# A softcap attention and a mixture of attention experts on one core: one batch's second score slot a step sooner, the second head pair's operands copied out in three pieces, and other constants in the order's search

## The chip, the cores and the metric

The kernel runs on one core of a Trainium2 chip. A core has a matrix engine (TensorE; PE in the profile, its weight loads PEld), a vector engine (VectorE, DVE), a scalar engine for activation functions (ScalarE, ACT), a general engine (GpSimd, POOL) and a queue engine that starts most transfers (SyncE, SP). The metric is the device time of one execution in microseconds (us); less is better. Of several runs of a kernel the median counts.

## The reference

Attention with a soft cap comes first, for 8 batches of 12 heads, 448 positions and 64 numbers a head:

```python
scores = q @ k.T / 8
scores = cap * tanh(scores / cap)          # cap = 30
attn = exp(scores - max) / sum             # over the keys
x = attn @ v                               # then heads side by side: (8, 448, 768)
```

Its output is the input of a mixture of four attention experts with 64 numbers each. A gate (x by a 768 x 4 matrix) picks two experts for each position, with weights w0 and w1 from a softmax over the two; each expert is a causal attention over x with projections of its own:

```python
for e in range(4):
    q, k, v = x @ wq[e], x @ wk[e], x @ wv[e]
    a = softmax(causal(q @ k.T / 8))
    out += weight_of_e * (a @ v) @ wo[e]   # weight 0 where e isn't chosen
```

So each score of the first attention costs ScalarE a tanh and an exp, and each of the second costs an exp. The experts of a batch need all twelve heads of that batch.

## The kernel before, in words

**Heads in pairs.** The 96 heads are taken as 48 pairs p = 0 to 47, six pairs a batch. The last batch begins with pair 42. For each of its pairs only the first 320 rows of queries are done pair by pair; the last 128 rows of all six come as two further steps, p = 48 and p = 49, called groups here, with three pairs each.

For each p the scores are filled into PSUM by TensorE in three parts, by chunks of keys. X is the first 128 keys of both heads and the tails (the last 64 keys of both heads side by side), Y1 and Y2 the second and third 128 keys of both. ScalarE takes a tanh of each part as it copies it to SBUF (`tanh`, line 842). Then one exp runs over the whole pair (`expo`, line 854). X owns three PSUM banks and Y two, so a part can be filled only when the tanh of what was there before is done. `fill` gives these matmuls (lines 789 in `heads` and 799 in `tails`). In general Y2 of pair p and X of pair p + 1 are filled by one operation of the program. The set `alone` lists the p for which they are two operations: pair 0, and every p with a slot (below).

Before a pair's scores can be filled, its operands must be brought: loads by SyncE, casts to 16 bits on GpSimd and VectorE (`cast`; the keys' tail is the cast at line 681), TensorE's transposes, and VectorE's copies to the tile qk (`tr`; keys 512 columns and queries 448 columns, 960 in all). Pair 0 has a branch of its own with several copies (lines 724 and 761). For the others up to pair 33 all transposes go to one PSUM bank and one copy of 960 columns follows (line 752). `setup_v` zeroes the padding of the value tiles (the memsets at lines 526 to 531).

After the exp of a pair, TensorE does its product with the values (`pv`, lines 869 and 877), VectorE normalises (lines 898 and 901) and the result is transposed (`xt`) to xT, the experts' input.

**The experts of a batch** are worked in beside the next batch's pairs: `b_v` (values and gate), `b_qk` (queries and keys), `b_gate`, `b_mask`. A batch has two *slots* of scores, s = 0 and 1: for each position the first chosen expert and the second, with the queries of the others masked to zero. `b_score` fills 18 matmuls into two of the X banks (line 1158), and one exp on ScalarE (line 1167) takes them; then come ten products with the values (`b_pv`, line 1217), the normalising with the gate's weights (line 1232), a sum of the two slots and transposes (`b_ot`) and the output projection (`b_wo`, line 1279; two matmuls make one pair for half of 128 rows, copied out at line 383). Slots stand at offsets 5 and 6 from the batch's end: for batch b at p = 6(b + 1) + 5 and + 6. Batch 6 has offsets 5 and 7 by the table `late`, so p = 47 and p = 49.

In the loop over p, the order of ScalarE's work at a step with a slot is: tanh of X and Y1 of p, the exp of pair p - 1, the slot's exp, tanh of Y2 of p. So a fixed chain of ScalarE's instructions is written down by the order of the calls.

**The last batch's experts** have no pairs to stand beside. `last` does the first 320 rows (projections line 1372, scores 1401, exp 1430, products 1458), with ScalarE and VectorE sharing the copies. `last2` does the last 128 rows (scores 1518, products 1572). `normed` normalises a block of 128 rows (lines 1308 to 1316), transposes it to oTL, does the output projection (line 1345) and the stores (lines 1354 to 1361).

**The planner.** No instruction is issued as the functions run. They record operations in a `Graph`, with the engine, an estimated duration, what is read and written, and PSUM groups. `dues` gives each operation a due time backwards from ScalarE's chain; some calls state it as an offset from a tanh (the pairs `(ref, offset)`). `solve` (line 134) then simulates the engines and issues in the order that results. On each engine it takes among the operations that can start within `near` the one that ranks first (`rank`, line 190). Score fills, transposes and a few others are `first`: ranked by their due times as they are, while all others are ranked no earlier than 1.097 us from now. A group already begun gets a bonus of 0.796, a second half-array matmul (scores) one of 2.0. `SEEDS` and `JIT` shift the ranks by a pseudo-random amount for each 4 us. At the end, a `first` operation that can start soon passes ahead of the one chosen if it would be due within 0.433 us of that one's end (line 206):

```python
for t2, u in c:
    if u.first and u.due + lag < t + o.occ + 0.433 and t2 < t + (
            o.occ if early else max(SWITCH + 0.01, min(o.occ, 0.25))):
        t, o = t2, u
        break
```

All this happens while the program is built; the chip sees only the order on each engine and the waits.

Of the kernel before, what the change touches and what calls it, by code (L numbers as in the profile page):

```python
# [18 lines left out]
TAIL = 4  # L19
LAND = 2.942  # L20
LAND0 = 2.314
FLIGHT = 8
JIT = 0.377
SEEDS = (0, 0, 0, 641, 0, 564, 447, 0, 424, 0, 460, 0, 235, 957, 407, 782, 983, 0, 912, 404, 0, 970, 362, 0, 379, 864, 0, 72, 966, 0, 904, 104, 0, 980, 497, 974, 196, 827, 159, 0, 805, 165, 0, 235, 0, 755, 596, 262, 998, 26, 102, 0, 0, 552, 777, 594, 0, 873, 143, 97, 0, 0, 943, 0, 690, 925, 0, 147, 0, 0, 0, 830, 464, 0, 0, 0, 267, 0)
TWIRE = 0.1
# [28 lines left out]
class Graph:  # L54
# [79 lines left out]
    def solve(self, when, banks, lent):  # L134
# [44 lines left out]
        while len(order) < n:  # L179
            best = None  # L180
            for e, rs in ready.items():
                if not rs:
                    continue
                c = [(est(o, e), o) for o in rs if e == o.eng or not left]
                if not c:
                    continue
                t0 = min(x[0] for x in c)
                if t0 >= INF or (best is not None and t0 >= best[0]):
                    continue
                def rank(x):  # L190
                    u = x[1]
                    if u.name[:4] == "gexp":
                        return -INF, 0.0, 0
                    d = u.due + lag if u.first or left < TAIL else max(u.due + lag, t0 + 1.097)
                    d -= 0.796 * (u.grp is not None and not u.opens and left >= TAIL)
                    k = SEEDS[int(t0 / 4.0)] if t0 < 4.0 * len(SEEDS) else 0
                    if k:
                        d += ((u.idx * 40503 + k * 9973) % 1009 / 1009.0 - 0.5) * JIT
                    return d - 2.0 * (u.half == 1 and half == 1), u.due, u.idx

                near = t0 + (0.005 if left >= TAIL else SWITCH + 0.02)
                t, o = min((x for x in c if x[0] <= near), key=rank)
                early = e == "POOL" and t < HEAD
                if (e in ("PE", "DVE") or early) and not o.first:
                    for t2, u in c:
                        if u.first and u.due + lag < t + o.occ + 0.433 and t2 < t + (
                                o.occ if early else max(SWITCH + 0.01, min(o.occ, 0.25))):
                            t, o = t2, u
                            break
                if best is None or t < best[0]:  # L210
                    best = (t, e, o)
# [64 lines left out]
def kernel(  # L276
# [85 lines left out]
    def bank16(g):  # L362
        return BANK[g.bank].bitcast(f16)
# [331 lines left out]
    def tr(p):  # L695
# [19 lines left out]
        if p == 0:  # L715
# [10 lines left out]
                name="qk0")  # L726
            return
        g = Group(AUX)
        if p >= KD:
# [12 lines left out]
            return  # L742
        pe(0, lambda: tk(g, (0, 1, 2)), kr + [("s", XB[0])] * (p == 1), [("tps", p, "k"), ("qkw", t)], g, occ=0.165, name=f"trk{p}")
        m, kx = (4, (-1,)) if p == 1 else (2, ())
        pe(0, lambda: (tq(g, 0, m), None if kx else tk(g, (-1,))),
           [("q16", i), "ident"] + (ktr if not kx else []),
           [("tps", p, "q")], g, occ=0.2 if kx else 0.15, name=f"trq{p}",
           due=5.0 if p == 1 else None)
        pe(0, lambda: tk(g, kx) if kx else tq(g, 2, 4), [("q16", i), "ident"] + (ktr if kx else []),
           [("tps", p, "r")], g, occ=0.06 if kx else 0.1, name=f"trr{p}" if p == 1 else "", due=5.0 if p == 1 else None)  # L750
        dve(c_dve(S + 512, True),
# [231 lines left out]
    def b_v(b, ref):  # L983
        x = b % 2
        for n in range(4):
            g = Group(AUX + XB, 1.8)
            w = WIN[n]
            for j0 in (0, 2, 4):
                def mm(g=g, w=w, j0=j0):
# [18 lines left out]
    def b_qk(b, ref):  # L1008
        x = b % 2
        for r in range(2):  # L1010
            for which in "kq":
                g = Group(AUX + XB, 2.4)
                w2 = (wq2 if which == "q" else wk2)[r]
                for j in range(NDC):
                    def mm(g=g, w2=w2, j=j, which=which):
# [348 lines left out]
    def last(ref):  # L1364
# [82 lines left out]
        for n in range(3):  # L1447
# [5 lines left out]
            def mm(g=g, n=n):  # L1453
                for e in range(E):
# [57 lines left out]
    def last2(ref):  # L1512
# [83 lines left out]
    for p in range(NPV):  # L1596
# [13 lines left out]
        for what in order:  # L1610
            if what == "Y2" and p:
# [96 lines left out]
```

## Time and profile before

| | |
|---|---|
| three runs | 305.9, 306.69, 307.45 us; median 306.69 |
| the profiled execution | 306.74 us |
| its span in the trace | 304.7 us |
| instructions | 8981 |
| busy share of the span: PE, PEld | 92%, 62% |
| DVE, ACT, POOL | 70%, 95%, 61% |
| TensorE's granted clock, mean | 1.0 |
| exp of the pairs (line 854), 51 instructions | 142.7 us |
| tanh of Y and X (line 842), 100 and 50 | 101.7 and 68.5 us |

The span is what the trace covers, from the first instruction to the last transfer's end. The execution's own time is 306.74 us, about 2 us more, and that is what the runs' times are to be compared with. Busy shares are means over the whole span; they say which engine has room on the whole, but not in which stretch. In a row of a timeline stand the start in us from the span's beginning, the busy time, engine, line, operation, the tile written and the tile read, the shape, how many instructions the row holds (x4), and in brackets the engine's idle time just before with what ended it. Matmuls overlap, so the ends of their rows are later than the start of the next.

### The profile page before, as it was taken

How to read it: one execution, taken by the hardware profiler on the slowest of the kernel's cores; microseconds unless marked ns; L12 is line 12 of the kernel's file. 1: busy time of each engine (PE TensorE's matmuls, PEld its weight loads, DVE VectorE, ACT ScalarE, POOL GpSimd, SP SyncE). 2: the span in 40 equal slices, each digit the busy share in tenths (PEclk: the TensorE clock that was granted, in tenths of full speed). 3: DMA queues.
4: the chain of work that ended last, by engine and by line, in shares of the span. 5: the costliest groups of instructions: out<-in, count | busy, mean ns of one | idle time of the engine just before them, and what ended most of it. 6: DMA issues, size and time to landing. Idle time of an engine off the chain costs nothing.

```text
span 304.7 us, 8981 instructions
## 1 busy us (share of the span) xinstructions
PE 278.8 (92%) x3488; PEld 187.7 (62%) x3488; DVE 212.0 (70%) x643; ACT 290.8 (95%) x246; POOL 184.3 (61%) x513
## 2 busy tenths in 40 slices
PE   7886679999999999999999999999998889999993
PEld 3553446676657776667666676556665566667761
DVE  2354656776658886687867876688865887586883
ACT  5999999999999999999999999999999999999682
POOL 6696244899859674967689463945568332920420
PEclk9999999999999999999999999999999999999999
DMA  6799999999993599559995662539137950553127
GB/s 184 167 239 229 238 268 255 237 254 228 250 271 79 170 258 250 131 149 308 254 219 149 219 198 62 129 88 238 25 63 71 208 131 20 81 163 93 37 103 261
DMA packets 86874, 53.12 MB, mean 174 GB/s; under 512 B 47536, under 2 KB 83120, under 8 KB 86832
## 3 DMA queue, kind: packets, MB, share of 16 engines
q1 hardware_dynamic: 86528, 52.33, 68.9%
q8 instruction: 27, 0.44, 0.6%
q10 hardware_dynamic: 304, 0.23, 0.2%
q14 instruction: 15, 0.12, 0.2%
HBM read 36.19 MB, written 11.01 MB: 155 GB/s over the span
## 4 chain that ended last, share of the span: by engine, by line
ACT 83%; PE 7%; issue 3%; DMA 2%; DVE 1%; SPq 1%; POOL 1%; DVEq 0%; ACTq 0%; POOLq 0%
ACT yp L842 42%; ACT yp L854 37%; ACT pP L1167 5%; DMA kf<-in_k_dram 2%; PE A L1279 1%; PE Y0s L1518 0%; PE A L1345 0%; PE A L1372 0%; PE Y L789 0%; SPq L490 0%; PE X0X1s L1158 0%; SPq L495 0%; SPq L486 0%; PE X0s L1401 0%; PE A L1401 0%
## 5 line engine op out<-in xcount | busy, mean ns | idle before, releaser
L854 ACT ACTIVATE yp<-yp 128x3136 f16<-128x3136 f16 (+4 forms) x51 | 142.7, 2801 | 0.0
L842 ACT ACTIVATE yp<-Y 128x896 f16<-128x896 f32 (+2 forms) x100 | 101.7, 1017 | 1.1 <-PE Y L789 1.1
L842 ACT ACTIVATE yp<-X 128x1344 f16<-128x1344 f32 (+2 forms) x50 | 68.5, 1370 | 0.4 <-PE X L799 0.4
L877 PE MATMUL A<-v,yp 128*128 128x65 f16 x1116 | 55.5, 193 | 0.0
L877 PEld LDWEIGHTS <-yp 128*128 128x128 f16 x1116 | 48.4, 97 | 5.6 <-issue 3.7
L869 PE MATMUL A<-vtz,yp 128*128 128x130 f16 x186 | 41.3, 222 | 7.9 <-ACT yp L854 4.7
L901 DVE TENSOR_TENSOR xk<-A,rca 128x256 f16<-128x256 f32 (+1 forms) x96 | 39.5, 414 | 2.5
L651 POOL CAST q<-qf 112x512 f16<-112x512 f32 x44 | 26.7, 618 | 9.4 <-PE A L701 6.3
L687 POOL CAST v<-vf 128x384 f16<-128x384 f32 x48 | 24.3, 509 | 10.7 <-PE A L877 6.4
L898 DVE RECIPROCAL rca<-A 128x4 f32<-128x4 f32 (+1 forms) x96 | 17.1, 178 | 19.5 <-PE A L877 17.9
L869 PEld LDWEIGHTS <-yp 128*128 128x128 f16 x186 | 18.0, 97 | 20.5 <-ACT yp L854 9.3
L383 DVE COPY ob<-A 128x384 f32<-128x384 f32 (+1 forms) x50 | 26.4, 553 | 5.8 <-PE A L1279 5.1
L752 DVE COPY qk<-A 128x960 f16<-128x960 f16 x33 | 21.2, 653 | 10.0 <-PE A L701 8.5
L789 PE MATMUL Y<-qk 64*128 64x448 f16 x136 | 24.7, 357 | 2.3 <-ACT yp L842 1.7
L1232 DVE SCALAR_TENSOR_TENSOR oB<-A,rcb,mw 128x256 f16<-128x256 f32 x54 | 25.1, 479 | 1.1
L1279 PE MATMUL A<-wo,oT 128*128 128x384 f16 x108 | 24.2, 326 | 1.4 <-DVE ob L383 0.6
L636 POOL CAST k<-kf 128x384 f16<-128x384 f32 x33 | 16.6, 514 | 14.4 <-DMA kf<-in_k_dram 10.2
L1177 POOL TENSOR_SCALAR_AFFINE_SELECT pP<-pP 128x384 f16<-128x384 f16 x14 | 7.4, 527 | 29.4 <-ACT pP L1167 20.2
L1217 PE MATMUL A<-vB,pP 128*128 128x260 f16 x134 | 22.0, 274 | 0.9 <-DVE oB L1232 0.4
L701 PE MATMUL A<-ident,q 112*128 112x112 f16 x192 | 20.8, 212 | 1.5 <-POOL q L651 0.6
L991 PE MATMUL A<-wvg,xT 128*128 128x260 f16 x168 | 21.9, 274 | 0.0
L1242 POOL TENSOR_TENSOR oS<-oB,oB 128x512 f16<-128x512 f16 x14 | 16.2, 1154 | 6.1 <-issue 4.3
(231 smaller groups left out, 591.8 us busy)
## 6 DMA issues: line engine op xcount, KB each, us to landing
qf<-in_q_dram SPq DMA_DIRECT2D x23, 448.0 KB, 6.5
kf<-in_k_dram SPq DMA_DIRECT2D x23, 384.0 KB, 5.8
vf<-in_v_dram SPq DMA_DIRECT2D x23, 384.0 KB, 4.8
out_dram<-ob SPq DMA_DIRECT2D x21, 384.0 KB, 3.1
ktf<-in_k_dram SPq DMA_DIRECT2D x46, 32.0 KB, 5.3
vtf<-in_v_dram SPq DMA_DIRECT2D x46, 32.0 KB, 4.5
out_dram<-ob SPq DMA_DIRECT2D x6, 192.0 KB, 3.1
ob<-in_moe_wv_dram SPq DMA_DIRECT2D x2, 384.0 KB, 4.5
```

What stands on the lines that cost most here:

```text
L383: (nc.scalar.copy if o.eng == "ACT" else nc.vector.tensor_copy)(dst(), src())
L651: e(q16[i], qf[s][:, h].rearrange("p h (c d) -> p c h d", c=QC))
L687: nc.gpsimd.tensor_copy(v16[u][:, :, :, 0:Dh], vf[s][:, h].rearrange("p h (c d) -> p h c d", c=KC))
L789: nc.tensor.matmul(dst[:, g, o], kT[r, 128 * (c + 1) : 128 * (c + 2)], t[r, qs], start=True, stop=True,)
L842: ACTS[what, p] = act(c_act(n * (b - a)), lambda: nc.scalar.activation(y[:, a:b, 0:n], src[:, 0 : b - a, 0:n], AF.Tanh, scale=isc / capf), ...
L854: act(c_act(n * (b - a), False), lambda a=a, b=b, n=n: nc.scalar.activation(y[:, a:b, 0:n], y[:, a:b, 0:n], AF.Exp, scale=capf), ks, ks, f ...
L869: nc.tensor.matmul(ps[:, n, :, :], y[:, 2 * S + w : 2 * S + w + 128], vtz[u], start=(n == 0), stop=False, skip_group_check=True,)
L877: nc.tensor.matmul(ps[:, n, h, :], y[:, o : o + 128], v16[u][:, h, c, :], start=False, stop=(c == 2), skip_group_check=True,)
L901: dve(c_dve(128 * m), lambda g=g, i=i, rc=rc, m=m: nc.vector.tensor_tensor(xk[p % NXK][:, 2 * i : 2 * i + m, :, :], view(g)[:, 0:m, :, 0:D ...
L1217: nc.tensor.matmul(bank(g)[:, 0 : E * (Dh + 1)], pB[pi][:, o : o + 128], vB[x][:, c, :, :], start=(t == 0), stop=(t == len(cs) - 1),)
L1232: dve(c_dve(E * Dh) + 0.06, lambda g=g, k_=k_, n=n: nc.vector.scalar_tensor_tensor(oB[s][:, n, :, :], view(g)[:, :, 0:Dh], rcb[k_][:, 0, : ...
L1279: nc.tensor.matmul(bank(g)[:, 0 : D // 2], oT[x][:, n // 2, r, n % 2, :], wo2[r][:, c0:c1], start=(r == 0), stop=(r == 1),)
```

## The change

1. **Pair 1's operands.** `tr` gets a branch for p = 1: keys, queries and the tail keys are transposed into three PSUM groups and copied by three operations (384, 448 and 128 columns), where one copy of 960 columns followed all transposes.
2. **Pair 1's Y2** is filled by an operation of its own (1 joins `alone`), no longer together with pair 2's X.
3. **Batch 6's second slot** stands at p = 48, not 49 (`late` is empty).
4. **The planner's constants**: the look-ahead of line 206 is 0.0 for 0.433, and those of rank, of `near`, of the jitter, of a transfer's assumed landing and of six due offsets are others. With them the order of nearly all work on TensorE, VectorE, GpSimd and SyncE moves somewhat, while ScalarE's fixed chain is the same but for point 3.

```diff
-LAND = 2.942
+LAND = 3.509
-JIT = 0.377
-SEEDS = (0, 0, 0, 641, 0, 564, 447, 0, 424, ...)
+JIT = 0.507
+SEEDS = (0, 0, 0, 941, 246, 328, 366, 428, 291, ...)
...
-                    d = u.due + lag if u.first or left < TAIL else max(u.due + lag, t0 + 1.097)
-                    d -= 0.796 * (u.grp is not None and not u.opens and left >= TAIL)
+                    d = u.due + lag if u.first or left < TAIL else max(u.due + lag, t0 + 0.423)
+                    d -= 2.838 * (u.grp is not None and not u.opens and left >= TAIL)
...
-                    return d - 2.0 * (u.half == 1 and half == 1), u.due, u.idx
-                near = t0 + (0.005 if left >= TAIL else SWITCH + 0.02)
+                    return d - 7.518 * (u.half == 1 and half == 1), u.due, u.idx
+                near = t0 + (0.023 if left >= TAIL else SWITCH + 0.02)
...
-                        if u.first and u.due + lag < t + o.occ + 0.433 and t2 < t + (
+                        if u.first and u.due + lag < t + o.occ + 0.0 and t2 < t + (
...
+        if p == 1:
+            for a, z_, fn, r_, y, o_ in (
+                    (S + 128, S + 512, lambda g: tk(g, (0, 1, 2)), kr + [("s", XB[0])], "k", 0.165),
+                    (0, S, lambda g: tq(g, 0, 4), [("q16", i), "ident"], "q", 0.2),
+                    (S, S + 128, lambda g: tk(g, (-1,)), ["ident"] + ktr, "t", 0.06)):
+                g = Group(AUX)
+                pe(0, lambda g=g, fn=fn: fn(g), r_, [("tps", p, y), ("qkw", t)], g, occ=o_,
+                   name=f"tr{y}{p}", due=5.0)
+                dve(c_dve(z_ - a, True), lambda g=g, a=a, z_=z_: nc.vector.tensor_copy(
+                    qk[t][:, a:z_], bank16(g)[:, a:z_]), [("tps", p, y)], [("qk", t, y)], g,
+                    name=f"qk{p}")
+            return
...
-    late = {6: (5, 7)}
+    late = {}
-    alone = {0, *exps}
+    alone = {0, 1, *exps}
...
-                   due=(ref, 7.244 + 1.4 * n))                                      # b_v
+                   due=(ref, 3.402 + 1.4 * n))
-                        due=(ref, 11.984 + 5.015 * r + 1.8 * (which == "q")))       # b_qk
+                        due=(ref, 18.023 + 2.606 * r + 2.868 * (which == "q")))
-                   [(b, 3, "z")]), None, WIN1[n], (ref, 9.616))                     # last
+                   [(b, 3, "z")]), None, WIN1[n], (ref, 8.582))
-               gt2[3][:, 1, 0], W1, (ref, 9.108))                                   # last2
+               gt2[3][:, 1, 0], W1, (ref, 11.239))
-                xt(p - 1, (ACTS["Y1", p], 3.335))
+                xt(p - 1, (ACTS["Y1", p], 4.132))
-                        b_wo(bb, ACTS["Y1", p], *((19.451, 1.8) if bb < LB - 1 else (10.566, 0.5)))
+                        b_wo(bb, ACTS["Y1", p], *((25.546, 1.8) if bb < LB - 1 else (18.614, 0.5)))
```

The old branches for p = 1 inside the general path of `tr` (lines 743 to 750) fall away with the new one.

More of the change, by code (lines that the diff above doesn't have):

```diff
@@ L19 @@
 TAIL = 4
-LAND = 2.942
+LAND = 3.509
 LAND0 = 2.314
 FLIGHT = 8
-JIT = 0.377
-SEEDS = (0, 0, 0, 641, 0, 564, 447, 0, 424, 0, 460, 0, 235, 957, 407, 782, 983, 0, 912, 404, 0, 970, 362, 0, 379, 864, 0, 72, 966, 0, 904, 104, 0, 980, 497, 974, 196, 827, 159, 0, 805, 165, 0, 235, 0, 755, 596, 262, 998, 26, 102, 0, 0, 552, 777, 594, 0, 873, 143, 97, 0, 0, 943, 0, 690, 925, 0, 147, 0, 0, 0, 830, 464, 0, 0, 0, 267, 0)
+JIT = 0.507
+SEEDS = (0, 0, 0, 941, 246, 328, 366, 428, 291, 367, 0, 549, 975, 0, 873, 0, 863, 234, 323, 966, 107, 394, 684, 804, 292, 881, 629, 223, 646, 0, 599, 0, 822, 0, 356, 956, 126, 289, 0, 72, 0, 369, 0, 164, 207, 0, 464, 467, 593, 0, 510, 0, 405, 803, 651, 0, 760, 527, 0, 0, 290, 44, 836, 337, 392, 178, 0, 828, 0, 328, 0, 886, 297, 356, 72, 991, 71, 10)
 TWIRE = 0.1
@@ L742, in tr @@
             return
[L743 to L750, printed above, removed]
+        pe(0, lambda: tk(g, (0, 1, 2)), kr, [("tps", p, "k"), ("qkw", t)], g, occ=0.165, name=f"trk{p}")
+        pe(0, lambda: (tq(g, 0, 2), tk(g, (-1,))), [("q16", i), "ident"] + ktr,
+           [("tps", p, "q")], g, occ=0.15, name=f"trq{p}")
+        pe(0, lambda: tq(g, 2, 4), [("q16", i), "ident"], [("tps", p, "r")], g, occ=0.1)
         dve(c_dve(S + 512, True),
```

## The prediction

> **What bounds the kernel now.** I read the page first, then busy time by stage, then ScalarE's timeline at both ends, then those of the other engines there. The page, with the span and the chain of work that ended last, by engine:
>
> ```profile
> span 304.7 us, 8981 instructions
> ...
> ACT 83%; PE 7%; issue 3%; DMA 2%; DVE 1%; SPq 1%; POOL 1%; DVEq 0%; ACTq 0%; POOLq 0%
> ```
>
> ScalarE is the chain. The stages (length, then busy us of PE, weight load, DVE, ACT and POOL, the granted clock, DMA share and GB/s) say where it is not:
>
> ```profile
> 14.00:60.00 46.00, 38.28 (x453) 22.76 (x454) 26.56 (x76) 45.74 (x35) 27.28 (x94) 1.00 1.03 247
> 60.00:278.50 218.50, 208.55 (x2664) 143.62 (x2660) 164.35 (x490) 218.50 (x172) 142.45 (x363) 1.00 0.67 166
> 278.50:284.80 6.30, 6.15 (x98) 4.85 (x98) 4.11 (x19) 6.30 (x6) 0.78 (x3) 1.00 0.05 11
> 284.80:296.00 11.20, 11.20 (x158) 8.04 (x155) 8.73 (x36) 7.63 (x21) 4.88 (x9) 1.00 0.18 54
> 296.00:304.70 8.70, 3.65 (x28) 1.94 (x24) 4.08 (x14) 2.20 (x5) 0.00 (x0) 0.99 0.76 279
> ```
>
> From 14 to 284.8 us ScalarE idles 0.26 us in all (46.00 less 45.74; the two stages behind it are full). So the time is three pieces: a head, some 270 us of ScalarE work that the change neither adds to nor takes from, and a tail of 20 us after ScalarE's last tanh and exp, where TensorE is busy to 296. Only head and tail can be won; the middle can only be lost. The execution took 306.74 us, 2.0 more than its span; the three runs' median is 306.69, the same within 0.05.
>
> **The head.** ScalarE's timeline there, with the idle time and what ended it in brackets:
>
> ```profile
> 9.26 1.29 ACT L842 ACTIVATE yp<-X 128x1344 f16<-128x1344 f32 x1 [0.39 <-PE X L799]
> ...
> 14.32 0.92 ACT L842 ACTIVATE yp<-Y 128x896 f16<-128x896 f32 x1 [0.26 <-PE Y L789]
> 15.13 1.28 ACT L842 ACTIVATE yp<-X 128x1344 f16<-128x1344 f32 x1
> ```
>
> 0.39 is pair 1's X waiting for its operands. 0.26 is pair 1's Y2, whose fill is one operation with pair 2's X and so waits for pair 2's operands. The change touches both. GpSimd, VectorE and TensorE ahead of them:
>
> ```profile
> 7.08 0.30 POOL L681 CAST ktz<-ktf 128x128 f16<-128x128 f32 x1
> 7.31 0.22 POOL L529 MEMSET vtz<- 128x130 f16 x1
> 7.59 0.23 POOL L531 MEMSET vtz<- 64x1 f16 x2
> ...
> 12.83 0.53 POOL L681 CAST ktz<-ktf 128x128 f16<-128x128 f32 x2
> ```
> ```profile
> 5.11 0.39 DVE L724 COPY qk<-A 128x448 f16<-128x448 f16 x1 [0.47 <-PE A L701]
> 5.42 0.22 DVE L761 COPY qk<-A 128x128 f16<-128x128 f16 x1
> ...
> 7.83 0.66 DVE L752 COPY qk<-A 128x960 f16<-128x960 f16 x1 [0.95 <-PE A L711]
> ...
> 13.54 1.22 DVE L752 COPY qk<-A 128x960 f16<-128x960 f16 x2 [0.92 <-PE A L701]
> ```
> ```profile
> 8.86 0.36 PE L799 MATMUL X<-qk 128*128 128x448 f16 x1
> ...
> 14.55 0.36 PE L799 MATMUL X<-qk 128*128 128x448 f16 x1
> ```
>
> One 0.66 us copy after the last transpose becomes three: 0.39 (448 wide), 0.22 (128 wide) and one of 384, which the trace does not show and which I put between those two, at 0.36. That is 0.97 for 0.66, 0.3 more on VectorE, which waits 0.95 there: hidden, and if that cover went, 0.3 would be paid. Keys and queries are copied while the tail keys are still cast; only the 0.22 copy stands behind the last transpose, where 0.66 does now. But the new order puts two vtz steps (7.31 to 7.82, 0.51 us) ahead of the tail-key cast, which starts at 7.08 now. I take all of it for the slip: cast from 7.59 to 7.89, transposed by 8.3, copied by 8.55, so that pair 1's X is filled 0.3 sooner than at 8.86. The 0.39 becomes 0.1.
>
> The 0.26 at 14.32 goes, since pair 1's Y2 needs only pair 1 now. What is late next is pair 2's X. Its tail keys are cast at 12.83 in both orders (the same steps stand ahead of the cast), the copy ends at 13.54 + 0.66 = 14.2, its last matmul at 14.55 + 0.36 = 14.91, so its tanh starts near 14.95 instead of 15.13. What pair 1 gains ahead of this is waited for here. **The head gives 0.18 us**; between -0.3 (the copies are paid) and 0.65 (both waits gone).
>
> **The tail.** Batch 6's second slot moves from group 49 to 48 (two groups hold the last 128 rows of the last batch's pairs): its 18 score matmuls and its exp go ahead of group 48's Y2, its ten PV matmuls follow. ScalarE has the same instructions, so it ends 0.18 sooner. What changes is TensorE's load behind it. Rows of TensorE, in order of start:
>
> ```profile
> 276.42 0.22 PE L869 MATMUL A<-vtz,yp 128*128 128x130 f16 x1 [0.41 <-DVE oB L1232]
> ...
> 278.52 0.34 PE L789 MATMUL Y<-qk,kd 64*128 64x128 f16 x6
> 278.79 0.63 PE L1158 MATMUL X0X1s<-qm,kB 128*128 128x128 f16 x10
> 279.26 0.30 PE L1372 MATMUL A<-xT,wq 128*128 128x320 f16 x1
> ...
> 284.10 0.61 PE L1217 MATMUL X1s<-vB,pP 128*128 128x260 f16 x4
> 284.55 0.22 PE L948 MATMUL Y1s<-vtz,yp 128*128 128x130 f16 x1
> ...
> 293.70 0.81 PE L1279 MATMUL A<-wo,oT 128*128 128x384 f16 x4
> 294.35 0.26 PE L1572 MATMUL X0s<-vB,yp 128*128 128x65 f16 x3
> ```
>
> Matmuls overlap, so I cost them by distances of starts: ten score matmuls 0.47 (278.79 to 279.26), a PV matmul of 260 columns 0.113 (four in 0.45), a pair of output matmuls 0.325 (four in 0.65). Behind the last Y2 fill (278.52) stand ten score matmuls and all ten PV matmuls now, and none in the new order: 0.47 + 1.13 = **1.60 us less**. They run where TensorE has room: it sat 0.41 us for a VectorE copy at 276.42. Against it, batch 6's exp now precedes the Y2 tanhs of both groups, so the last fill comes later by that exp less the head's gain:
>
> ```profile
> 270.53 1.14 ACT L1167 ACTIVATE pP<-X 128x1024 f16<-128x1024 f32 x1
> 271.43 0.83 ACT L842 ACTIVATE yp<-Y 128x640 f16<-128x640 f32 x1
> ```
>
> The exp is 0.90 to the next start; 0.90 - 0.18 = 0.72 later. Of 1.60, 0.9 remains at the end of TensorE's work, if its waits stay as they are.
>
> They do not quite, since the order of the last matmuls changes too. Behind the PV of the last batch's last rows (L1572, 294.35) now stand 2 pairs of L1279, 8 pairs of L1345 and 24 other PV matmuls (L1458); in the new order 4 pairs of L1279, 2 of L1345 and one pair of transposes. So L1572 itself runs later: 9.8 us of matmuls stand between the last PV of group 49 and it, instead of 8.2. That PV ends at 284.55 + 0.22 = 284.77; with 9.8, and 1.1 more for waits on VectorE's normalising steps (an estimate; 284.77 + 8.2 = 292.97 against 294.35 shows 1.4 of waits now), L1572 comes near 295.7. A chain follows it, in the rows of now:
>
> ```profile
> 295.81 0.41 DVE L1316 TENSOR_TENSOR oB<-X0s,slL 128x256 f16<-128x256 f32 x1
> ...
> 297.76 0.22 DVE L383 COPY oTL<-A 128x128 f16<-128x128 f16 x1
> 298.11 2.32 DVE L383 COPY kf<-A 128x384 f32<-128x384 f32 x4
> ```
> ```profile
> 300.99 0.59 SPq L1361 DMA_DIRECT2D out_dram<-kf  x1
> ```
>
> From the last L1572 to its product's end it is 296.22 - 294.6 = 1.6 now, and I take 1.75, since output copies stand between: 297.45. From there to the end of the last oTL copy 0.95: 298.4 (two transposes, hand-overs and a copy of 0.22 as at 297.76, with a wait). Two pairs of output matmuls, 0.65: 299.05. The last two copies are then split between VectorE and ScalarE (now four stand on VectorE, 298.11 to 300.43): both end near 299.55, and the two last stores are issued from two queues at once, by 299.6, where now the last issue is 300.99. From that issue to the end of the span it is 304.7 - 300.99 = 3.7 us, and I keep that: 303.3; with two halves landing side by side perhaps 0.2 less. **The tail and head give 1.4 to 1.6 us** in this sum: 306.74 - 1.6 = **305.1 us**. Bounds of the tail: nothing, if the later L1572 eats the 0.9 and the stores, and 2.6 (1.60, and the 1.0 from 299.99 to 300.99 that three pairs of output matmuls less on the end save).
>
> [...]
>
> **The rivals.** *TensorE is not the bound of the tail.* For it: weight loads fill 72% of the stage from 284.8 to 296, and 1.4 us of it were waits in that sum. Against it: the matmul row is busy for all 11.20. If it holds, the 0.9 is not paid, and the later L1572 costs its own chain: only 0.3 of the end is left, 306.4.
>
> *More than the sum.* The 1.1 of waits on VectorE shrinks to a third, and nothing stands between the last steps of the chain: 1.2 more, 303.9.
>
> *ScalarE waits in the middle (the slower side).* The old order let a score fill pass ahead of another matmul group if it was due within 0.433 us of that group's end; the new one within 0. One pair of output matmuls (0.325) may then stand ahead of a due fill. Rows of a tight place:
>
> ```profile
> 83.52 0.36 PE L789 MATMUL Y<-qk 64*128 64x448 f16 x2
> ```
> ```profile
> 83.92 1.15 ACT L842 ACTIVATE yp<-Y 128x896 f16<-128x896 f32 x1
> ```
>
> The fill ends at 83.88, its tanh starts at 83.92: 0.04 to spare. Each late fill costs 0.325 - 0.04 = 0.29 us. Six eat up the gain; eleven pass 0.5%. There are some 148 fills: one late in ten, 15, costs 4.3, net 2.7 slower, 309.4. Against it: adding up the matmuls between each fill and the next, no stretch of the new order holds more than ScalarE's time above it, but the first slot of batch 0 (4.12 of 4.35, added up by distances of starts as above) comes near; and later pairs' transposes stand further ahead.
>
> *The change does not do what it says:* the moved exp finds its scores unready. Rows of ScalarE and VectorE around its new place:
>
> ```profile
> 272.10 1.18 ACT L842 ACTIVATE yp<-X 128x1152 f16<-128x1152 f32 x1
> ...
> 275.78 0.86 ACT L842 ACTIVATE yp<-Y 128x768 f16<-128x768 f32 x1
> ```
> ```profile
> 268.65 0.60 DVE L1036 TENSOR_TENSOR qm<-A,mT 128x448 f16<-128x448 f32 x1
> ```
>
> The X banks are free at 273.3, the exp is due at 275.78 - 0.18 = 275.6: 2.3 us for 18 score matmuls (0.047 each: 0.85) beside the PV of the pair before, and their last operand, qm, is ready at 269.3. I give it no chance of its own; in part it would look like the first rival, since the exp's lateness is at most one or two tenths.
>
> **How the numbers follow.** Forecast 305.1 (304.6 to 305.7): 0.46, of which a little over half lies more than 0.5% under 306.69, that is under 305.16 (half a per cent is about what a measurement of this kernel can tell from no change). More than the sum, 303.9 to 304.6: 0.20. TensorE not the bound, 306.4 (305.7 to 307.2): 0.16. ScalarE waits, above 308.2: 0.18. Faster 0.25 + 0.20 = 0.45, same 0.21 + 0.16 = 0.37, slower 0.18. The range, 303.9 to 307.4, leaves out the last case and the far end of the second.
>
> **What would show it.** In the new profile: the idle times of 0.39 and 0.26 in the head become about 0.1 and some tenths ahead of pair 2's X; ScalarE busy without a gap from 15 to 284.6; the score exp ahead of the first Y2 tanh near 275.6; the 2.00 us of idle time that ScalarE has ahead of the last batch's first key copy shrinks; L1572 near 295.7; the two last copies side by side and the last issue by 299.6. Waits of ScalarE between 60 and 278 prove the slower case; L1572 before 295 the second; a last issue after 300.5 the first.

## The result: 0.6% slower

The new kernel takes 308.22 us (median of 7 runs, 307.8 to 309.14), the one before 306.87 us (7 runs, 305.9 to 307.45): a ratio of 1.0056, 95% interval 1.0034 to 1.0079. A second measurement (after_again in the table below) gave 308.28 us and 1.0053 (1.0028 to 1.0079). Three of the new kernel's seven runs stand at 309.1 us and four at 307.8 to 308.2, and the mean granted clock does not tell them apart (0.982 to 0.986 and 0.984 to 0.989). Forecast was 305.1, with a range up to 307.4.

The page of the new kernel's profiled execution, with its span and the chain that ended last, then its stages, in the columns of the prediction:

```profile
span 306.1 us, 8982 instructions
...
ACT 67%; PE 20%; DVE 5%; issue 4%; POOL 2%; DVEq 0%; POOLq 0%
```
```profile
14.00:60.00 46.00, 38.13 (x464) 23.73 (x465) 26.42 (x78) 46.00 (x35) 26.23 (x88) 0.93 0.95 241
60.00:278.50 218.50, 209.07 (x2665) 144.03 (x2662) 166.74 (x487) 218.36 (x171) 141.49 (x362) 1.00 0.67 166
278.50:284.80 6.30, 6.30 (x102) 4.78 (x101) 5.78 (x25) 6.08 (x7) 2.26 (x2) 1.00 0.33 43
284.80:296.00 11.20, 10.90 (x134) 7.38 (x131) 7.77 (x34) 7.88 (x22) 2.54 (x7) 1.00 0.03 7
296.00:306.10 10.10, 3.02 (x31) 1.56 (x29) 2.85 (x8) 2.15 (x5) 0.00 (x0) 0.85 0.79 273
```

ScalarE idles 0.14 us in the middle (46.00 of 46.00 busy, 218.36 of 218.50), so next to nothing was lost there. The head gained. ScalarE's timeline of the new kernel (the line numbers are eight higher behind the new branch: L842 is L850 here, L1572 is L1580, L1279 is L1287):

```profile
9.15 1.29 ACT L850 ACTIVATE yp<-X 128x1344 f16<-128x1344 f32 x1
...
13.84 0.92 ACT L850 ACTIVATE yp<-Y 128x896 f16<-128x896 f32 x1
14.63 1.30 ACT L850 ACTIVATE yp<-X 128x1344 f16<-128x1344 f32 x1
...
281.71 2.62 ACT L862 ACTIVATE yp<-yp 128x1920 f16<-128x1920 f16 x2
284.56 0.42 ACT L383 CAST kB<-X0s 128x320 f16<-128x320 f32 x1 [0.22 <-PE X0s L1380]
```

The waits of 0.39 and 0.26 are both gone, pair 2's X starts at 14.63 instead of 15.13, and the last exp of the chain at 281.71 instead of 282.20. The 2.00 us that ScalarE waited for the last batch's first key copy are 0.22. Up to here this execution is ahead of the profiled one of the kernel before.

How much of the 0.50 is the change's is less sure, since the two waits are not there in every execution of the old order. Three further runs of the kernel before, with nothing edited ahead of the tail (b_small_ob, b_one and b_inter below), have neither. b_inter:

```profile
6.50 0.92 ACT L842 ACTIVATE yp<-Y 128x896 f16<-128x896 f32 x1 [1.34 <-PE Y L789]
...
9.51 1.29 ACT L842 ACTIVATE yp<-X 128x1344 f16<-128x1344 f32 x1
...
14.20 0.92 ACT L842 ACTIVATE yp<-Y 128x896 f16<-128x896 f32 x1
15.00 1.30 ACT L842 ACTIVATE yp<-X 128x1344 f16<-128x1344 f32 x1
```

ScalarE's first tanh starts at 5.95 in the execution that the prediction read, at 6.50 to 6.86 in these three; the waits show only where it was early. Pair 2's X starts at 15.00 to 15.35 in the four profiles of the old order and at 14.49 to 15.09 in seven of the new one (the new kernel, after_again, a_small_ob, a_cut64, a_cut128, a_one and a_inter): 0.36 sooner in the mean.

Now the tail: the queue's own rows for SyncE, and ScalarE's last issue, in the new kernel, then SyncE's in the one before. (SPq and ACTq are the queues of SyncE and ScalarE; `ob` holds batch 6's output, `kf` the last batch's and, in one 64-row store, batch 6's.)

```profile
295.15 0.36 SPq L1301 DMA_DIRECT2D out_dram<-ob  x1
295.60 0.38 SPq L1369 DMA_DIRECT2D out_dram<-kf  x1
296.36 0.47 SPq L1366 DMA_DIRECT2D out_dram<-kf  x1
296.92 1.27 SPq L1369 DMA_DIRECT2D out_dram<-kf  x2
298.28 1.56 SPq L1301 DMA_DIRECT2D out_dram<-ob  x2
299.93 0.75 SPq L1362 DMA_DIRECT2D out_dram<-kf  x1
...
300.12 0.35 ACTq L1362 DMA_DIRECT2D out_dram<-kf  x1
```
```profile
294.36 2.95 SPq L1293 DMA_DIRECT2D out_dram<-ob  x3
297.74 0.33 SPq L1361 DMA_DIRECT2D out_dram<-kf  x1
298.70 0.33 SPq L1354 DMA_DIRECT2D out_dram<-kf  x1
299.59 0.33 SPq L1361 DMA_DIRECT2D out_dram<-kf  x1
300.46 0.48 SPq L1358 DMA_DIRECT2D out_dram<-kf  x1
```

TensorE's last four output matmuls, in the new kernel and in the one before, start almost together:

```profile
298.75 0.82 PE L1353 MATMUL A<-wo,oTL 128*128 128x384 f16 x4
```
```profile
298.89 0.81 PE L1345 MATMUL A<-wo,oTL 128*128 128x384 f16 x4
```

With the issue at 300.99 that the prediction shows, the kernel before ends 3.7 us behind its last issue. The new one issues its last store 0.87 us sooner, at 300.12, and ends 6.0 us behind it: 0.87 gained, 2.27 lost, 1.4 on the span (306.1 for 304.7). The busy time by windows shows why, first the new kernel, then the one before; the last two columns are the DMA engines' busy share and GB/s:

```profile
296.00:297.60 1.60, 1.27 (x21) 0.85 (x20) 1.44 (x5) 0.94 (x3) 0.00 (x0) 1.00 1.03 413
297.60:299.20 1.60, 1.38 (x9) 0.71 (x9) 0.84 (x3) 0.73 (x2) 0.00 (x0) 1.00 0.99 232
299.20:303.60 4.40, 0.37 (x3) 0.00 (x0) 0.57 (x2) 0.48 (x1) 0.00 (x0) 0.95 1.00 366
303.60:304.00 0.40, 0.00 (x0) 0.00 (x0) 0.00 (x0) 0.00 (x0) 0.00 (x0) 0.50 0.40 146
304.00:304.40 0.40, 0.00 (x0) 0.00 (x0) 0.00 (x0) 0.00 (x0) 0.00 (x0) 0.50 0.26 96
304.40:304.80 0.40, 0.00 (x0) 0.00 (x0) 0.00 (x0) 0.00 (x0) 0.00 (x0) 0.50 0.11 38
304.80:306.10 1.30, 0.00 (x0) 0.00 (x0) 0.00 (x0) 0.00 (x0) 0.00 (x0) 0.50 0.00 0
```
```profile
295.20:297.20 2.00, 2.00 (x33) 1.53 (x32) 1.87 (x10) 1.22 (x3) 0.00 (x0) 1.00 0.98 392
297.20:297.80 0.60, 0.55 (x6) 0.28 (x5) 0.55 (x4) 0.51 (x2) 0.00 (x0) 1.00 0.02 5
297.80:301.60 3.80, 1.90 (x12) 0.93 (x10) 2.33 (x5) 0.96 (x2) 0.00 (x0) 1.00 1.01 396
301.60:303.20 1.60, 0.00 (x0) 0.00 (x0) 0.00 (x0) 0.00 (x0) 0.00 (x0) 1.00 0.98 282
```

From 296 on the DMA engines are full in the new kernel, without a gap, until 303.6, and the last of them ends at 304.8, when every compute engine has been idle for over 4 us. In the kernel before they had a gap at 297.2, with the three stores of batch 6 gone, before the last batch's stores came. The same 2688 KB (3 x 384, 2 x 384, 4 x 192) are issued within 6.6 us there and within 5.0 us here. To leave as fast as they are issued, they would need over 540 GB/s here; the best row shows 413. And in one stretch, 297.6 to 299.2, the rate falls to 232 at a full share.

### The profile page after: what moved, and what is told of

It is laid out like the page before. It is cut to its first block, busy times and chain, and to the rows that moved or that the text cites. A ratio compares the mean times of both kernels' runs of the same rounds, so it can differ in the third digit from the quotient of the medians.

```text
span 306.1 us, 8982 instructions
## 1 busy us (share of the span) xinstructions
PE 279.6 (91%) x3488; PEld 188.8 (62%) x3488; DVE 214.6 (70%) x644; ACT 290.9 (95%) x247; POOL 183.4 (60%) x513
## 4 chain that ended last, share of the span: by engine, by line
ACT 67%; PE 20%; DVE 5%; issue 4%; POOL 2%; DVEq 0%; POOLq 0%
ACT yp L850 35%; ACT yp L862 28%; ACT pP L1175 4%; PE A L885 2%; PE Y L797 2%; PE A L1287 2%; PE A L1026 2%; PE A L877 1%; PE X L1166 1%; PE A L1597 1%; DVE oB L1240 1%; PE A L999 1%; PE A L701 1%; PE X L807 1%; PE A L1353 1%
## 5 line engine op out<-in xcount | busy, mean ns | idle before, releaser
L850 ACT ACTIVATE yp<-Y 128x896 f16<-128x896 f32 (+2 forms) x100 | 100.0, 1000 | 1.3 <-PE Y L797 1.3
L850 ACT ACTIVATE yp<-X 128x1344 f16<-128x1344 f32 (+2 forms) x50 | 67.7, 1355 | 0.1
L885 PEld LDWEIGHTS <-yp 128*128 128x128 f16 x1116 | 49.1, 98 | 5.7 <-issue 4.0
L877 PEld LDWEIGHTS <-yp 128*128 128x128 f16 x186 | 18.1, 97 | 21.1 <-ACT yp L862 9.9
L797 PE MATMUL Y<-qk 64*128 64x448 f16 x136 | 25.4, 369 | 2.6 <-ACT yp L850 2.3
L760 DVE COPY qk<-A 128x960 f16<-128x960 f16 x32 | 20.5, 652 | 6.1 <-PE A L701 5.9
L1287 PE MATMUL A<-wo,oT 128*128 128x384 f16 x108 | 23.5, 325 | 0.5 <-DVE oB L1324 0.4
L939 DVE COPY xT<-A 128x448 f16<-128x448 f16 (+1 forms) x38 | 14.6, 385 | 11.1 <-PE A L930 10.6
L1026 PE MATMUL A<-xT,wq 128*128 128x64 f16 (+1 forms) x168 | 19.7, 260 | 0.7 <-DVE oB L1240 0.4
```

The lines of the kernel that those rows point to most:

```text
L797: nc.tensor.matmul(dst[:, g, o], kT[r, 128 * (c + 1) : 128 * (c + 2)], t[r, qs], start=True, stop=True,)
L850: ACTS[what, p] = act(c_act(n * (b - a)), lambda: nc.scalar.activation(y[:, a:b, 0:n], src[:, 0 : b - a, 0:n], AF.Tanh, scale=isc / capf), ...
L877: nc.tensor.matmul(ps[:, n, :, :], y[:, 2 * S + w : 2 * S + w + 128], vtz[u], start=(n == 0), stop=False, skip_group_check=True,)
L885: nc.tensor.matmul(ps[:, n, h, :], y[:, o : o + 128], v16[u][:, h, c, :], start=False, stop=(c == 2), skip_group_check=True,)
L1026: nc.tensor.matmul(bank(g)[:, o : o + t.stop - t.start], w2[:, j, :], xT[x][:, j, t], start=(j == 0 and o == 0), stop=(j == NDC - 1), skip ...
L1287: nc.tensor.matmul(bank(g)[:, 0 : D // 2], oT[x][:, n // 2, r, n % 2, :], wo2[r][:, c0:c1], start=(r == 0), stop=(r == 1),)
```

## The experiments

Two theories at first. **D** (drain): the last stores wait behind the bytes of those ahead of them. **T** (TensorE): the order of the last matmuls sets the end, and a store takes a fixed time. Later **R**: a store from 64 rows drains at half rate; and **P** against **F** on its reason. All runs in one table. Names that begin with a are edits of the new kernel, those with b of the one before; after_again is the new kernel unchanged. The ratio is to the kernel before measured beside the run, whose medians were 306.5 to 306.9; "last issue" is that of either queue, "rest" the time from it to the end of the span, both in the one profiled execution of the run.

| run | us | ratio (95%) | last issue | rest |
|---|---|---|---|---|
| before | 306.5 to 306.9 | 1 | 300.99 | 3.7 |
| new kernel | 308.22 | 1.0056 (1.0034 to 1.0079) | 300.12 | 6.0 |
| after_again | 308.28 | 1.0053 (1.0028 to 1.0079) | 300.28 | 5.9 |
| a_small_ob | 305.77 | 0.9953 (0.9929 to 0.9977) | 299.99 | 3.6 |
| b_small_ob | 306.57 | 0.9994 (0.9973 to 1.0016) | 300.89 | 3.6 |
| a_wo_due | 308.42 | 1.0043 (1.0012 to 1.0074) | 302.90 | 3.5 |
| a_wo_mid | 308.76 | 1.0069 (1.0040 to 1.0099) | 302.38 | 4.8 |
| a_cut64 | 305.71 | 0.9969 (0.9945 to 0.9992) | 300.20 | 3.6 |
| a_cut128 | 307.79 | 1.0039 (1.0019 to 1.0059) | 301.52 | 5.4 |
| a_one | 313.80 | 1.0231 (1.0202 to 1.0261) | 300.67 | 12.0 |
| b_one | 313.86 | 1.0227 (1.0198 to 1.0256) | 300.45 | 11.6 |
| a_inter | 306.22 | 0.9985 (0.9957 to 1.0012) | 300.31 | 4.3 |
| b_inter | 305.97 | 0.9973 (0.9947 to 0.9999) | 300.57 | 3.2 |
| b_split | 312.35 | 1.0182 (1.0114 to 1.0251) | 306.83 | 3.9 |
| b_late | 308.50 | 1.0065 (1.0046 to 1.0084) | 303.01 | 4.0 |
| a_tail | 308.42 | 1.0063 (1.0050 to 1.0076) | 302.39 | 4.2 |
| a_tail2 | 307.80 | 1.0043 (1.0027 to 1.0058) | 302.33 | 3.7 |
| a_late | 310.38 | 1.0123 (1.0110 to 1.0137) | 302.32 | 6.6 |

**Bytes out of the drain (a_small_ob, b_small_ob).** The order on every engine stays, only the size of three stores changes:

```diff
-  out[b, w + lo : w + 128, :], o[lo:128, :]                  # b_wo, all batches
+  out[b, w + (lo if b < LB - 1 else 120) : w + 128, :], ...  # batch 6: 8 rows for 128
```

> The new kernel, but batch 6's three 128-row output stores write 8 rows each instead of 128 (120 rows of each are left out of the output). Instructions and their order on every engine stay as they are; 3 x 360 KB of the 2.69 MB that are stored at the end are gone. Theory D (drain: the last stores wait behind the bytes of those ahead of them): the last issue stays near 300.1 us, what follows it falls from 6.0 to about 3.8 us, span 303.9 and time about 306.0, 2.2 less than the new kernel. Theory T (TensorE's order and the chain of the last products set the end, a store then takes its fixed time): nothing changes, 308.2.

> The kernel before with the same cut (batch 6's three 128-row stores write 8 rows each, 120 rows of each left out). Theory D: those stores go out from 294.4 and the DMA share falls to 0.30 at 297 to 298, so their backlog is gone before the last batch's stores begin; 0 to 0.4 us less than before, 306.5 to 306.9; with the cut in both, the new kernel is then 0.5 to 0.9 faster, by its earlier last issue (300.12 against 300.99). Theory T: nothing changes here either, and the new kernel stays 1.3 slower.

D holds in both. The new kernel without those bytes takes 305.77, its rest 3.6 us; the kernel before without them is unchanged (306.57). With these bytes left out of both, the new kernel is 0.8 us the faster by the medians, as its earlier last issue says. T falls as the reason for the loss.

**The same bytes earlier (a_wo_due, a_wo_mid).**

```diff
-  b_wo(bb, ACTS["Y1", p], *((25.546, 1.8) if bb < LB - 1 else (18.614, 0.5)))
+  b_wo(bb, ACTS["Y1", p], *((25.546, 1.8) if bb < LB - 1 else (10.566, 0.5)))   # a_wo_due
+  b_wo(bb, ACTS["Y1", p], *((25.546, 1.8) if bb < LB - 1 else (15.0, 1.0)))     # a_wo_mid
```

> The new kernel with one constant of before: the due offset of batch 6's output projection, 10.566 for 18.614. The planner then puts its 12 matmuls ahead of the last batch's scores instead of among its last products, and the three 128-row stores go out while the DMA engines are idle (they are from 285 to 295). Theory D: 1.8 to 2.4 us less than the new kernel, about 306.0; stores of the last batch land in 2.6 us instead of 3.4 to 4.8. Theory T: TensorE has the same work before the last product; the 8 matmuls that move from behind the last batch's last PV to ahead of it shift that PV by 1.3 us and save 1.3 behind it: 308.0.

> The new kernel with the due times of batch 6's output projection between the two (offset 15.0 and step 1.0 for 18.614 and 0.5): 5 of its 6 pairs of matmuls stand ahead of the last batch's last PV (2 in the new kernel, 6 in the run with offset 10.566), all behind the first scores of the last batch. Theory D+T (the later of two sets the end: TensorE's chain plus 3.75 us, or the drain of the stores): three pairs more ahead of the last PV are 3 x 0.325 = 1.0 on the chain, less what they filled of waits behind it, so the last issue at 300.4 to 301.1; stores begin 1 to 2 us earlier, and from the last issue to the end 3.8 to 4.3 us instead of 6.0; time 306.2 to 307.0, 1.2 to 2.0 less than the new kernel and level with the one before. Theory D alone (only the drain counts): 305.5. Theory T alone: 308.2 to 308.8.

D alone missed both, and the sum of the two missed a_wo_mid. The drain went as D says in a_wo_due (rest 3.5) and in part in a_wo_mid (4.8, where 3.8 to 4.3 was expected), but the last issue came 2.3 to 2.8 us later, where 1.0 was the most that had been reckoned; T's numbers are near only because the two changes cancel. ScalarE's rows of a_wo_due:

```profile
286.07 0.42 ACT L383 CAST kB<-A 128x320 f16<-128x320 f32 x1 [1.74 <-PE A L1380]
```
```profile
289.21 0.44 ACT L1438 ACTIVATE pP<-A 128x320 f16<-128x320 f32 x1 [0.67 <-PE A L1428]
```

Its first key copy comes at 286.07 (284.56 in the new kernel) and its first exp of the last batch at 289.21 (285.67): pairs of output matmuls put ahead of the last batch's projections and scores hold up everything behind. T is right that TensorE's order bounds the tail too here; the end is the later of the two. The earlier stores bought nothing (308.42 and 308.76), since TensorE paid for them.

**Which bytes (a_cut64, a_cut128).** The same number of bytes (372 KB) out of different stores, the order unchanged:

```diff
-  out[LB - 1, KM:S, :], o[0:64, :]            # and the last batch's o[64:128, :]
+  out[LB - 1, KM : KM + 2, :], o[0:2, :]      # a_cut64: both 64-row stores, 2 rows each
-  out[b, w + lo : w + 128, :], o[lo:128, :]
+  out[b, w + lo : w + (4 if b == LB - 1 and n == 2 else 128), :], ...   # a_cut128
```

> The new kernel, its order unchanged, but the two 64-row stores of the last blocks write 2 rows each (372 KB less; 62 rows of each are left out of the output). In the stretch where these drain (297.6 to 299.2) the DMA share stays at 1.0 while the rate falls from 400 to 154 GB/s. Theory R (a store from 64 rows drains at half rate or less): these 372 KB cost about 1.9 us, time 306.2 to 306.5. Theory B (bytes alone count): 372 KB at 390 GB/s, 0.95 us, 307.2.

> The new kernel, its order unchanged, but one 128-row store of batch 6 (its third) writes 4 rows (372 KB less; 124 rows are left out of the output). The same bytes as the cut of the two 64-row stores. Theories R and B: 0.95 us less by bytes at 390 GB/s, 307.2. Theory T: 308.2.

R holds, and more than it asked: with nearly all of the two 64-row stores left out the time is 305.71, 2.6 us under after_again by the ratios (0.9969 against 1.0053), where 1.9 was reckoned. The same bytes out of a 128-row store are worth 0.4 (1.0039), half of what was reckoned for them and not clear of nothing, since the intervals overlap. The drain of a_cut64:

```profile
296.00:302.20 6.20, 3.11 (x32) 1.58 (x29) 2.94 (x8) 2.23 (x5) 0.00 (x0) 0.97 0.97 379
302.20:302.60 0.40, 0.00 (x0) 0.00 (x0) 0.00 (x0) 0.00 (x0) 0.00 (x0) 0.50 0.16 54
```

It ends 2.2 us sooner than the new kernel's (302.6 for 304.8). The stretch with 232 GB/s at a full share in the new kernel is gone here, so that is where those stores drain: the busy share, 0.99 there and 1.03 in the 413 GB/s just before, does not show it. In the slowest part of it the rate is well under half of the 400 around it, and why it is under half stays open:

```profile
298.40:298.80 0.40, 0.27 (x3) 0.06 (x2) 0.40 (x2) 0.29 (x1) 0.00 (x0) 1.00 1.16 154
```

**One store for two (a_one, b_one).** The two halves go to different places of the output; one store with two blocks of 64 rows writes both:

```diff
-  out[LB - 1, KM:S, :], o[0:64, :]
-  out[b, w0 + lo : w0 + 128, :], o[lo:128, :]
+  out.rearrange("b s d -> (b s) d")[b * S - 192 : (b + 1) * S, :]
+     .rearrange("(t r) d -> t r d", t=2)[:, 128:192, :], o
```

> The new kernel, its order on every engine unchanged, but the two 64-row stores of the last blocks become one store from 128 rows (the first of the two places issues nothing, the second issues both halves). The same bytes to the same places. Theory R (what stands behind the last issue is the slow drain of stores from 64 rows, and the stores queued behind them): the rate stays near 400 GB/s after 296.5, 2.69 MB drain in about 7 us, from the last issue to the end 3.8 to 4.5 us instead of 6.0, time 306.0 to 306.9. Theory D with bytes alone: 308.0 to 308.4, no change. This is a full kernel: under R it is level with the one before or ahead of it.

> The kernel before with the same edit; its two 64-row stores are its last two, issued at 300.46 and 300.99, with no store behind them. Theory R: one issue of 0.5 less and a faster drain of the last 384 KB, 0.5 to 1.0 us less than before: 305.6 to 306.1. Bytes alone: the issue time only, 0 to 0.5.

Both missed by 7 us, and not on R: the edit brought a cost of its own. Windows of a_one:

```profile
297.00:299.00 2.00, 1.58 (x17) 0.81 (x12) 1.18 (x5) 1.09 (x3) 0.00 (x0) 1.00 1.03 409
304.00:311.00 7.00, 0.00 (x0) 0.00 (x0) 0.00 (x0) 0.00 (x0) 0.00 (x0) 0.50 0.15 59
```

For 7 us the share is 0.15, hardly more than 2 of 16 engines, at 59 GB/s; in b_one it is 0.12 to 0.14 at 49 to 55 GB/s from 304 to 310. All 16 move 402 GB/s in a_inter below, 25 each, and by that 59 GB/s are 2.3 engines. The store's outermost dimension in the output is 2; that it ran on about two engines for that reason is the author's estimate, and no run tests it. R speaks of a low rate at a full share, and here the share itself is low. So a_one and b_one say nothing for or against R.

**Why the low rate (a_inter, b_inter).** The same stores with the same bytes, but the rows of the two halves interleaved over the partitions:

```diff
+  odd = slice(1, 128, 2) if n == 2 else slice(0, 128)
-  evac(256 - 2 * lo, lambda: oTL[u][:, :, lo:128], ...
+  evac(256 - 2 * lo, lambda: oTL[u][:, :, odd], ...
-  oTL[u][:, :, 0:64]                           # batch 6's columns
+  oTL[u][:, :, 0:128:2]
-  out[LB - 1, KM:S, :], o[0:64, :]
+  out[LB - 1, KM:S, :], o[0:128:2, :]          # and o[odd, :] for o[lo:128, :]
```

> The new kernel, its order on every engine unchanged, with the rows of the last mixed block interleaved: batch 6's 64 rows lie in the even partitions of the tile, the last batch's 64 rows in the odd ones, and the two 64-row stores take every second partition instead of one half each. Theory P (a store from one half of the partitions drains at half rate): the rate stays near 400 GB/s, from the last issue to the end 3.9 to 4.5 us instead of 6.0, time 306.2 to 306.9, level with the kernel before. Theory F (64 rows are too few rows, wherever they lie): 308.2, unchanged.

> The kernel before with the same interleaving; its two 64-row stores are the last two. Theory P: the last 384 KB drain in 1.0 us instead of 1.7, 0.5 to 0.8 us less than before, 305.8 to 306.1. Theory F: 306.6.

P holds in both. The drain of a_inter:

```profile
296.20:303.00 6.80, 3.02 (x31) 1.56 (x29) 2.85 (x8) 2.14 (x5) 0.00 (x0) 0.91 1.02 402
303.00:303.40 0.40, 0.00 (x0) 0.00 (x0) 0.00 (x0) 0.00 (x0) 0.00 (x0) 0.50 0.15 46
```

All bytes leave at 402 GB/s, and the drain ends 1.4 us sooner than in the new kernel. The time is 306.22, 2.1 less, level with the kernel before. So 1.7 of the 2.27 us by which the rest had grown come from where these 64 rows lie in the tile; some 0.6 stay (4.3 for 3.7), with the same bytes issued in less time. The kernel before with the same edit takes 305.97, a ratio of 0.9973 (0.9947 to 0.9999), its rest 3.2 for 3.7: the lowest median of a full kernel here, though only just clear of the kernel before and not clear of a_inter. With the interleaving in both, then, the change of this document shows no gain. What the two runs show is the place: with the 64 rows in partitions 0 to 63 and 64 to 127 the rate falls to 232 GB/s at a share of 0.99, and with the same rows in every second partition it stays at 402 (394 in b_inter). Why the rate falls there no run shows.

**The parts of the change alone.** b_split is the kernel before with the new branch of `tr` and 1 in `alone`; b_late has only `late = {}`; a_late is the new kernel with only `late = {6: (5, 7)}`; a_tail is a_late with the due times 10.566, 9.616 and 9.108 of before; a_tail2 is the new kernel with these due times.

> The kernel before with the head's edits alone: pair 1's operands in three copies, and its Y2 filled by itself. Where the new kernel's head gains by these edits: ScalarE reaches 20 us of its chain 0.2 to 0.5 us sooner, the tail is as before, 306.4 to 306.7. Where it gains by the constants' order: the idle times of 0.39 and 0.26 stay in part, 306.9.

> The kernel before with batch 6's second slot moved alone. By the prediction's step ten score matmuls and ten PV matmuls leave TensorE's queue behind the last Y2 fill, 1.60 us, of which 0.9 stays: 305.3 to 306.0, if no wait of ScalarE comes in the middle; the planner orders batch 6's output projection ahead of the last batch's first products here, so the stores go out early and nothing waits in the drain. If the move gains nothing by itself: 306.5 to 307.0.

> The new kernel with batch 6's second slot back in its old place, the due times as in the new kernel. The stores come in the order four of the last batch (the two of 64 rows second and fourth), two of batch 6, the last block, the third of batch 6. Theory R+T: the slot's 20 matmuls (1.6 us) are back behind the last Y2 fill and the stores of batch 6 wait for them, so this is slower than the new kernel: 308.5 to 310. If the slot's new place is what costs: 306.5 to 307.

> The new kernel with batch 6's second slot back in its old place and the three due times of the tail as before (10.566, 9.616, 9.108). Its tail's stores have the order of before: three of batch 6, then the last batch's with the two 64-row stores at the end; its first 4900 instructions on TensorE are those of the new kernel. If the whole loss is the tail: ScalarE's chain is 0.3 to 0.5 us ahead as in the new kernel, from the last issue to the end 3.7 us, and the time is 306.1 to 306.4, 0.3 to 0.5 less than before. If the constants cost something in the middle too: 306.7 or more, with waits of ScalarE between 15 and 280 us.

> The new kernel with the three due times of the tail as before (10.566, 9.616, 9.108), the slot in its new place. All of batch 6's output projection stands ahead of the last batch's scores here, so its stores go out while the DMA engines idle, and the 64-row stores are the last two. Theory R+T: nothing waits in the drain (3.7 to 4.0 us from the last issue to the end), but 6 pairs of matmuls (1.95 us) are ahead of the last batch's exps, as in the run of before with the slot alone, whose last issue came at 303.0: 307.5 to 308.5. By the prediction's step (1.60 us less on TensorE, 0.9 of it kept) with a tail in before's order: 305.3.

a_late came out on the side of R+T, a little beyond its numbers: undoing the slot costs 2.1 us (1.0123 against 1.0053), and the last issue is 2.2 later; the order of the stores is another there too. a_tail2 came within its first forecast: rest 3.7, last issue 302.33. The others missed. b_split lost 5.8 us, 4.4 of them to five waits of ScalarE in the middle, the longest of them here:

```profile
177.74 1.02 ACT L1179 ACTIVATE pP<-X 128x1024 f16<-128x1024 f32 x1 [3.27 <-POOL q L651]
```

With constants that were found for another program the planner's order leaves a slot's scores late: the prediction's slower rival at work, though here it is a slot's scores and a GpSimd cast (line 651) more than a Y fill. Its head has neither wait, but its pair 2's X starts at 15.23, within the range of the old order, so the head's edits alone gain nothing that one profile can tell. b_late and a_tail lost 1.9 each, mainly by TensorE's order in the tail (b_late has one wait of 0.48 in the middle, a_tail none): the last issue comes at 303.0 and 302.4. So moving the slot gains 2.1 us with the new constants (a_late) and loses 1.9 with the old ones (b_late): its worth hangs on the constants, and which of them is worth what stays open.

## Why the prediction was wrong

- **The head** was right in kind: 0.18 forecast, 0.50 measured between the two profiled executions, 0.36 in the mean of the profiles of the two orders. Two of its readings did not hold. The waits of 0.39 and 0.26 belong to one execution and not to the old order. And "Its tail keys are cast at 12.83 in both orders" is not so: the cast starts at 12.26 to 12.83 in the four profiles of the old order and at 11.19 to 12.87 in seven of the new one, so what pair 2's X waits for varies from one execution to the next.
- **The 1.60 us less behind the last Y2 fill** stand in the trace: the twenty matmuls that stood behind that fill are ahead of it, and it starts at 279.02, 0.50 later (0.72 forecast). But the step "Of 1.60, 0.9 remains at the end of TensorE's work" was mis-sized: TensorE's last four output matmuls start at 298.75, where they started at 298.89, and over the profiles of the two orders there is no lead at all (298.6 to 299.3 for the new one without a_cut128, where ScalarE had waited; 298.4 to 298.9 for the old one). Part of that was in the prediction: L1572 was forecast at 295.7 and came at 295.98.
- **The last issue** was forecast at 299.6 and came at 300.12, so 0.87 sooner than before. With TensorE only 0.14 ahead, this is mainly what the prediction says of the last two copies and stores: two engines and two queues share them, where the last store stood 0.53 behind another one on SyncE's queue (300.46 and 300.99).
- **ScalarE in the middle** does not wait; that rival did not occur in the new kernel. That 308.22 lies where the rival was priced (above 308.2) is a coincidence.
- **The failed step** is "From that issue to the end of the span it is 304.7 - 300.99 = 3.7 us, and I keep that". It was 6.0. With 3.7 the span would be 303.8 and the execution about 305.5; a_small_ob and a_cut64, where the rest is 3.6, measure 305.8 and 305.7. No row stands behind the 0.2 that the same sentence takes off for two halves landing side by side, and no run shows it. The prediction took a store's time as fixed; from issue to landing the medians of the last stores are 2.1 to 2.7 us in the kernel before and 3.4 to 4.8 in the new one. It had the row that said so: from 296 to 304.7 a DMA share of 0.76, which is 6.6 us of full engines in 8.7. Here 2688 KB were issued in 5.0 us and took 8.8 to leave (296 to 304.8), so a last issue 0.87 sooner did not end the tail sooner. And the change had put the two slow 64-row stores, the last two before, ahead of at least four others; a_inter, which leaves the order and gives these two stores the full rate, shows that their low rate in that place is most of the loss.
- **The rivals** were all about compute engines; none was the drain, and the range stopped at 307.4. Whether the weight loads' 72% or the matmul row's full 11.20 us measures TensorE's load in the tail no run shows; the 0.9 that the first rival left unpaid did not come (298.75 for 298.89).

## What to carry to other kernels

Before a tail is shortened, add up the bytes of its stores and divide by the best rate that the trace shows: that estimates the least time for the drain (here 2688 KB at 413 GB/s, 6.7 us, where it took 8.8), and a last issue 0.87 us sooner did not move it here. Read the GB/s beside the DMA share: here a share of 0.99 at 232 GB/s was two stores from one half of the partitions each, and interleaving their rows gave 402. A wait read in one execution need not be there in the next: look at a second one before it is priced. An edit in a kernel whose order comes from a search has to be judged with constants found for it: parts of the change alone cost 1.9 and 5.8 us here.

## What the runs showed of the hardware

TensorE's granted clock fell to 0.5 for some 3 to 4 us at a time, between 18 and 44 us (in the new kernel it is 0.50 in every half microsecond from 20 to 23 and from 37 to 40), at places that differ between executions of the same program (from about 20 and 37 us in the new kernel, from about 32 in after_again) and in some (the profiled ones of before, a_small_ob, b_one, b_inter, b_late and a_tail) not at all: their windows of 2 us stand at 1.00 from 12 to 62 us, and for b_inter and a_tail the mean clock is 0.996 and 0.998, where one fall would take off 0.006 (3.4 us at half the clock, of 304). TensorE's waits in the new kernel, and the two windows with the falls (the clock is the third number from the right):

```profile
PE A L877 <- ACT yp L862: 1.8, 1, 1.8
```
```profile
18.00:24.00 6.00, 4.50 (x51) 3.41 (x52) 1.93 (x6) 6.00 (x5) 4.04 (x18) 0.72 1.06 242
36.00:42.00 6.00, 4.77 (x45) 2.41 (x45) 1.75 (x6) 6.00 (x5) 3.06 (x8) 0.72 0.64 153
```

A wait of 1.8 us, in which TensorE had nothing to do, ends at 19.50, just ahead of the first fall; one of 2.19 ends at 36.80, ahead of the second. But one of 1.81 ends at 30.50 with no fall behind it, so the wait alone does not settle it, and what does stays open. Mostly this is covered, since ScalarE is the bound there (busy for 6.00 of 6.00 us in both windows); in a_cut128 a fall of 7 us (0.57 from 36 to 44) was not, and ScalarE waited 0.77 us for a Y fill at 44.58.
